# A decode-attention kernel whose last step is written out as a list of its own, and whose first output weights come in uneven pieces

## The chip, the cores and the metric

The kernel runs on one core of one Trainium2 chip. Its time is the device time of one execution in microseconds (us). A profile of one execution gives when every instruction and every DMA packet ran. The engines of the core are PE (the matrix engine; PEld is its loading of weights), DVE (vector), ACT (scalar, activation), POOL and SP, which here does nothing but issue DMAs.

## What is computed

One token goes through an attention block with a cached K and V, and through a gated feed-forward block; a sigmoid gate mixes the two. The cut reference:

```
def _A_ref(x, k_cache, v_cache, wq, wo):          # x 1x1x512, caches 1x32x65536x128, all bf16
    q = (x @ wq).reshape(1, 1, 32, 128).transpose(0, 2, 1, 3)
    scores = jnp.einsum("bhqd,bhkd->bhqk", q, k_cache) * (128 ** -0.5)
    p = softmax(scores)
    o = jnp.einsum("bhqk,bhkd->bhqd", p, v_cache)
    return o.transpose(0, 2, 1, 3).reshape(1, 1, 4096) @ wo

def _B_ref(x, w_gate, w_up, w_down):
    return (silu(x @ w_gate) * (x @ w_up)) @ w_down

g = sigmoid((x * gate_w).sum(-1, keepdims=True))
return g * a + (1 - g) * b
```

There are 32 heads of 65,536 keys and as many values of 128 numbers. K and V together are 1,074 MB, and each number is used once.

## The kernel before

**Tiles.** A head's 65,536 keys are four groups of 16,384; a group is a tile of 128 partitions x 128 keys x 128 numbers, 4,096 KB. Groups are counted through all heads, n = 0 to N-1 = 127, and h = n // 4. K comes in pairs of groups, m = 0 to M-1 = 63, into two slots of 64 KB a partition that are used in turn (`take`, `give`). V has one buffer of the same size, `V_buf`: a head's first pair comes in one DMA, its second pair one group at a time, as each half of the buffer comes free. For the last head the V of groups 124 and 127 goes into the second halves of the two K slots, which are free by then; their first halves hold `wo`, the output weights: heads 0 to 15 in the tile named `wo_early`, the later ones in `wo_late`.

**One group.** `products(n)` on DVE multiplies the K tile by the query (line 260) and adds the halves of each key's 128 products together until 32 are left (line 264, two instructions). `scores(n)` on PE sums these by eight matmuls with the identity (line 273). `fold(n)` on DVE sums the last four (line 288). After a head's four groups `row_max` takes the maximum (DVE line 294, ACT line 296, PE line 298), `exponentials` makes the weights P and their sum by partition (DVE line 303, ACT lines 305 and 307), `total` adds the sum over partitions on PE (line 315), and `weight` makes of it the factor of the head on DVE (lines 320 and 321). `values(n)` on PE multiplies P with the V tile in 32 matmuls (line 329) into one accumulator a head. `head_copy` (ACT line 343) and `head_turn` (PE line 359, ACT line 367) make a column of `oT` of it. At the end `project(h)` on PE multiplies each column with its head's rows of `wo`, in two matmuls of 256 columns into two accumulators (line 385).

**Order.** The order of all instructions on each engine is written out by hand: they run in program order there, and an engine waits where its next instruction's data isn't there. The loop is over i, a pair of groups a step, with `first` for a head's first pair. In a step DVE does `products(2i)`, a `fold` after its first instruction, `products(2i+1)`, another `fold`; PE does the `scores` of this pair and the `values` of the pair two before. In a `first` step the line `tot_ps = total(h - 1)` comes after both `values`, and DVE's `weight(h - 1)`, which reads it, between `products(2i+1)` and the next step's `products`. The last step is i = 63, with conditions of its own (`i == M - 1`), and what is left after it follows the loop.

**DMAs.** SP issues all the large ones in program order (lines 113, 182 and 184). A DMA signals its completion by sixteen marks on a semaphore. Eight semaphores take turns, so SP issues a DMA only when the eighth DMA before it has landed; it also waits until the readers of the place that is overwritten are done. `load_wo` brings heads in groups of four (`QUAD`), 4,096 bytes a partition and group: the 16 early heads in one DMA, the late ones by `LATE_CUTS`. V group 127 is cut into six DMAs (`V_CUTS`).

Of the kernel before, what the change touches and what calls it, by code (L numbers as in the profile page):

```python
# [8 lines left out]
ACT = mybir.ActivationFunctionType  # L9
ALU = mybir.AluOpType  # L10
AXIS = mybir.AxisListType
P = 128
# [3 lines left out]
NB = 128  # L16
# [7 lines left out]
TURNED = 8  # L24
V_CUTS = {3: (0, 64, NB), 2: (0, 64, NB), 1: (0, 32, 64, 96, 112, NB - TURNED, NB)}
EARLY = 16
LATE_CUTS = (EARLY, 24, 28, 30, 32)

GROUPED = 28


@with_exitstack
def kernel(
# [45 lines left out]
    def take(name):  # L79
        slot = free.pop(0)  # L80
        held[name] = slot
        return ring.tile(
            [P, PAIR * Dh], bf16, name=name.split(".")[0], tag=f"slot{slot}"
        )
# [36 lines left out]
    def load_v(n, half=0, spare=None):  # L121
        if n % G == 0 and spare is None:
            view = V_buf.rearrange("p (j d) -> p j d", d=Dh)
            V_tiles[n], V_tiles[n + 1] = view[:, :NB, :], view[:, NB:, :]
            load(view, A_v_cache, n // 2, (0, PAIR))
        else:
            view = V_buf if spare is None else spare
            view = view[:, half * NB * Dh : (half + 1) * NB * Dh]
            V_tiles[n] = view = view.rearrange("p (j d) -> p j d", d=Dh)
            load(view, A_v_cache, n // 2, V_CUTS.get(N - n, (0, NB)), n % 2 * NB)  # L130
# [17 lines left out]
    gval = consts.tile([P, 1], f32, name="gval")  # L148
    rg = consts.tile([P, H], f32, name="rg")
    HD = D // 2  # L150
    a_ps = [psum_a.tile([1, HD], f32, name=f"a{i}_ps") for i in range(2)]

    def queries():
        q_ps = psum_m.tile([P, H], f32, name="q_ps", tag="misc")
# [19 lines left out]
    def load_wo(tile, cuts):  # L174
        t = tile[:, : H * D].rearrange("p (h n) -> p h n", n=D)
        runs = t.rearrange("p (g j) n -> p g (j n)", j=QUAD)
        rows = A_wo.rearrange("(h p) n -> p h n", p=P)
        row_runs = A_wo.rearrange("(g p j) n -> p g (j n)", p=P, j=QUAD)
        for a, b in zip(cuts[:-1], cuts[1:]):
            if b <= GROUPED:  # L180
                a, b = a // QUAD, b // QUAD
                nc.sync.dma_start(out=runs[:, a:b, :], in_=row_runs[:, a:b, :])
            else:
                nc.sync.dma_start(out=t[:, a:b, :], in_=rows[:, a:b, :])
        return t
# [52 lines left out]
    def feed_forward_out(hT, rest):  # L238
        b_ps = psum_m.tile([1, D], f32, name="b_ps", tag="misc")
        for t in range(FT):  # L240
            nc.tensor.matmul(
                b_ps, lhsT=hT[:, t : t + 1], rhs=wd_sb[:, t, :], start=(t == 0), stop=(t == FT - 1)
            )
        b_sb = small.tile([1, D], f32, name="b_sb", tag="row", bufs=1)
        nc.scalar.activation(out=b_sb, in_=b_ps, func=ACT.Copy, scale=rest)
        for i, a in enumerate(a_ps):
            nc.tensor.matmul(
                a, lhsT=ones_f[0:1, 0:1], rhs=b_sb[:, i * HD : (i + 1) * HD], start=True, stop=False
            )

    def width_of(n):
        return FIRST if n < G else WIDTH
# [16 lines left out]
    def scores(n):  # L269
        S = F_tiles[n] = psum_s.tile([P, NB, QUAD], f32, name="S_ps")  # L270
        width = width_of(n)
        for c in range(0, width, QUAD):
            nc.tensor.matmul(  # L273
                S,
                lhsT=ident_b,
                rhs=K_tiles[n][:, :, c : c + QUAD],
                start=(c == 0),
                stop=(c == width - QUAD),
            )
        del K_tiles[n]  # L280
        if n % 2:
            give(f"K_t.{n // 2}")
# [9 lines left out]
    def row_max(h):  # L292
        m = small.tile([P, 1], f32, name="m")
        nc.vector.tensor_reduce(out=m, in_=S_tiles[h], axis=AXIS.X, op=ALU.max)  # L294
        diag = small.tile([P, P], f32, name="diag")
        nc.scalar.activation(out=diag, in_=ident_f, func=ACT.Copy, scale=m)  # L296
        mT_ps = psum_m.tile([P, P], f32, name="mT_ps", tag="misc")
        nc.tensor.matmul(mT_ps, lhsT=ones_f, rhs=diag, start=True, stop=True)  # L298
        return mT_ps

    def exponentials(h, mT_ps):
        top = small.tile([P, 1], f32, name="top")
        nc.vector.tensor_reduce(out=top, in_=mT_ps, axis=AXIS.X, op=ALU.max)  # L303
        bias = small.tile([P, 1], f32, name="bias")
        nc.scalar.activation(out=bias, in_=top, func=ACT.Copy, scale=-scale)  # L305
        P_tiles[h] = small.tile([P, NBH], bf16, name="P_sb")
        nc.scalar.activation(  # L307
            out=P_tiles[h], in_=S_tiles[h], func=ACT.Exp, bias=bias, scale=scale,
            accum_out=rowsum[:, h : h + 1],
        )  # L310
        del S_tiles[h]

    def total(h):
        tot_ps = psum_m.tile([P, 1], f32, name="tot_ps", tag="misc")
        nc.tensor.matmul(tot_ps, lhsT=ones_f, rhs=rowsum[:, h : h + 1], start=True, stop=True)  # L315
        return tot_ps
# [3 lines left out]
        nc.vector.reciprocal(recip, tot_ps)  # L320
        nc.vector.tensor_tensor(out=rg[:, h : h + 1], in0=recip, in1=gval, op=ALU.mult)

    def values(n):
        h, g = divmod(n, G)
        if g == 0:
            O_tiles[h] = psum_o.tile([4, 4 * Dh], f32, name="O_ps")
        end = NB if n < N - 1 else NB - TURNED
        for j in range(0, end, 4):
            nc.tensor.matmul(  # L329
                O_tiles[h],  # L330
                lhsT=P_tiles[h][:, g * NB + j : g * NB + j + 4],
                rhs=V_tiles[n][:, j : j + 4, :],
                start=(g == 0 and j == 0),
                stop=(g == G - 1 and j == end - 4),
            )
# [45 lines left out]
            )  # L381

    def project(h):
        for i, a in enumerate(a_ps):
            nc.tensor.matmul(  # L385
                a,
                lhsT=oT[:, h : h + 1],
                rhs=wo_sb[:, h, i * HD : (i + 1) * HD],
                start=False,
                stop=(h == H - 1),  # L390
            )


    queries()
# [5 lines left out]
    query(0)  # L400

    mT_ps = tot_ps = None
    for i in range(M):
        h, first = i // MH, i % MH == 0
        vector = products(2 * i)
        next(vector)
        if mT_ps is not None:
            exponentials(h - 1, mT_ps)
        if not first:
            fold(2 * i - 1)  # L410
        for _ in vector:
            pass
        if first or i == M - 1:
            scores(2 * i)
        if i >= 2:
            values(2 * i - 4)
            if first or i == M - 1:
                load_v(2 * i - 2 if first else N - 3)
        if not first and i < M - 1:
            scores(2 * i)  # L420
        if i == 0:
            xs = gate_sum()
            eg2 = gate_exp(xs)
        if i >= 2:
            values(2 * i - 3)
            if first or i == M - 1:
                load_v(2 * i - 1 if first else N - 2, 1)
            else:
                load_v(2 * i - 2)
        if mT_ps is not None:  # L430
            tot_ps = total(h - 1)
            mT_ps = None
        if first and i > MH:
            head_turn(h - 2, head_copy(h - 2))
        if i == 1:
            hT = feed_forward_mid(*ff)
            feed_forward_out(hT, rest)
            load_v(0)
        vector = products(2 * i + 1)
        next(vector)  # L440
        fold(2 * i)
        for _ in vector:
            pass
        if i == 0:
            rest = gate_value(eg2)
        if tot_ps is not None:
            weight(h - 1, tot_ps)
            tot_ps = None
        if not first and h + 1 < H:
            query(h + 1)  # L450
        scores(2 * i + 1)
        if i == 0:
            ff = feed_forward_in()
        if i + 2 < M:
            load_k(i + 2)
        elif i + 2 == M:
            spare = take("wo_early.0")
            wo_sb = load_wo(spare, (0, EARLY))
            load_v(N - 4, 1, spare)
        if not first:  # L460
            fold(2 * i + 1)
            mT_ps = row_max(h)
    spare = take("wo_late.0")
    load_v(N - 1, 1, spare)
    exponentials(H - 1, mT_ps)
    for o in range(EARLY):
        project(o)
    tot_ps = total(H - 1)
    head_turn(H - 2, head_copy(H - 2))
    values(N - 4)  # L470
    values(N - 3)
    weight(H - 1, tot_ps)
    wo_sb = load_wo(spare, LATE_CUTS)
    values(N - 2)
    values(N - 1)
    head_turn(H - 1, head_copy(H - 1))
    for h in range(EARLY, H):
        project(h)

    out_sb = small.tile([1, D], bf16, name="out_sb", bufs=1)  # L480
    nc.vector.tensor_copy(out=out_sb[:, :HD], in_=a_ps[0])  # L481
    nc.scalar.activation(out=out_sb[:, HD:], in_=a_ps[1], func=ACT.Copy)
    nc.sync.dma_start(out=out[0], in_=out_sb)


# [28 lines left out]
```

## Time and profile before

| What | us |
|---|---|
| Time, median of 3 runs (2524.94 to 2525.77) | 2525.67 |
| Time of the profiled execution | 2525.51 |
| Its span from the first to the last instruction | 2523.7 |
| PE busy | 1411.6 |
| DVE busy | 2066.2 |
| ACT busy | 115.2 |
| Read from HBM: 1087.64 MB, at 431 GB/s over the span | |
| Last matmul of `project` begins | 2520.9 |
| Output DMA is issued | 2521.65 |

Times within the execution are counted from the start of the span. The difference between the span and the execution's time, 1.8 us, lies around the span.

### The profile page before, as it was taken

What the parts mean: (1) busy time and instruction counts of PE and PEld (TensorE: products, weight loads), DVE (VectorE), ACT (ScalarE), POOL (GpSimd) and SP (SyncE); (2) the same over time, 40 slices, a digit from 0 to 9 for tenths busy, and PEclk for the clock granted to TensorE, in tenths of its full rate; (3) what the DMA queues carried; (4) which work ended last, traced back from release to release, by engine and by line L of the source; (5) the groups of instructions that cost most, each with busy time, mean ns of one, the idle gap of its engine ahead of it and who ended that gap; (6) DMA issues with size and microseconds to landing.
All of it is one profiled execution on the core that took longest, in us unless ns stands there. A gap on an engine that the chain in (4) does not pass through costs nothing.

```text
span 2523.7 us, 13226 instructions
## 1 busy us (share of the span) xinstructions
PE 1411.6 (56%) x5898; PEld 547.1 (22%) x5898; DVE 2066.2 (82%) x648; ACT 115.2 (5%) x348; POOL 0.7 (0%) x6
## 2 busy tenths in 40 slices
PE   3655654646646456555465464664545655546549
PEld 2211221212212122221122121221212222212214
DVE  5898888888888878889888888888788888987883
ACT  0000000000000000000000000000000000000000
POOL 0000000000000000000000000000000000000000
PEclk8777777777767777687787776876867777777779
DMA  9999999999999999999999999999999999999998
GB/s 415 436 434 434 438 432 429 436 433 436 431 431 432 435 442 433 431 427 435 437 434 432 429 437 434 437 435 428 431 437 437 434 433 427 440 431 433 433 430 363
DMA packets 26890, 1088.49 MB, mean 431 GB/s; under 512 B 3153, under 2 KB 3666, under 8 KB 4946
## 3 DMA queue, kind: packets, MB, share of 16 engines
q1 hardware_dynamic: 26546, 1087.65, 99.7%
q8 instruction: 46, 0.75, 0.1%
q14 instruction: 10, 0.08, 0.0%
q10 hardware_dynamic: 288, 0.00, 0.0%
HBM read 1087.64 MB, written 0.00 MB: 431 GB/s over the span
## 4 chain that ended last, share of the span: by engine, by line
DMA 62%; PE 33%; DVE 5%; issue 0%; another core or an unknown queue 0%; ACT 0%; SPq 0%; DVEq 0%; ACTq 0%
DMA V_buf<-in_A_v_cache_dram 58%; PE O_ps L329 29%; DMA K_t<-in_A_k_cache_dram 4%; PE S_ps L273 3%; DVE K_t L260 3%; DVE K_t L264 2%; PE a_ps L385 0%; PE oh_ps L359 0%; DVE S_sb L288 0%; PE tot_ps L315 0%; PE qb_ps L170 0%; DVE m L294 0%; DVE top L303 0%; ACT O_sb L343 0%
## 5 line engine op out<-in xcount | busy, mean ns | idle before, releaser
L260 DVE TENSOR_TENSOR K_t<-K_t,q_sb 128x16384 bf16<-128x16384 bf16 x128 | 1112.1, 8688 | 216.8 <-DMA K_t<-in_A_k_cache_dram 216.8
L329 PE MATMUL O_ps<-V_buf,P_sb 128*4 128x512 bf16 x4032 | 955.9, 400 | 356.3 <-DMA V_buf<-in_A_v_cache_dram 354.9
L264 DVE TENSOR_TENSOR K_t<-K_t 128x8192 bf16<-128x8192 bf16 x252 | 849.3, 3370 | 4.3
L273 PE MATMUL S_ps<-K_t,ident_b 128*128 128x512 bf16 x1056 | 358.6, 499 | 674.9 <-DVE K_t L264 674.9
L329 PEld LDWEIGHTS <-P_sb 128*4 128x4 bf16 x4094 | 358.0, 88 | 973.6 <-issue 507.9
L273 PEld LDWEIGHTS <-ident_b 128*128 128x128 bf16 x1056 | 117.7, 116 | 861.3 <-issue 783.4
L288 DVE TENSOR_REDUCE S_sb<-S_ps 128x128 f32<-128x512 f32 x128 | 87.7, 685 | 117.5 <-PE S_ps L273 117.5
L320 DVE RECIPROCAL recip<-tot_ps 128x1 f32<-128x1 f32 x32 | 5.4, 168 | 79.4 <-PE tot_ps L315 79.4
L376 ACT ACTIVATE oT<-oh_ps,rg 32x1 bf16<-32x1 f32 x112 | 28.6, 255 | 683.5 <-PE oh_ps L359 682.4
L298 PE MATMUL mT_ps<-diag,ones_f 128*128 128x128 f32 x64 | 21.5, 430 | 62.0 <-ACT diag L296 62.0
L172 ACT ACTIVATE q_sb<-qb_ps 128x128 bf16<-128x128 f32 x32 | 8.9, 277 | 933.4 <-PE qb_ps L170 933.4
L359 PE MATMUL oh_ps<-ident_f,O_sb 4*128 4x1 f32 x256 | 33.5, 248 | 0.5 <-ACT O_sb L343 0.5
L298 PEld LDWEIGHTS mT_ps<-diag,ones_f 128*128 128x128 f32 x64 | 13.4, 262 | 89.8 <-ACT diag L296 89.8
L359 PEld LDWEIGHTS oh_ps<-ident_f,O_sb 4*128 4x128 f32 x256 | 30.8, 186 | 1.0 <-ACT O_sb L343 0.5
L481 DVE CAST out_sb<-a_ps 1x256 bf16<-1x256 f32 x1 | 0.4, 413 | 33.2 <-PE a_ps L385 33.2
L296 ACT ACTIVATE diag<-ident_f,m 128x128 f32<-128x128 f32 x32 | 12.8, 401 | 308.0 <-DVE m L294 308.0
L307 ACT ACTIVATE P_sb<-S_sb,bias 128x512 bf16<-128x512 f32 x32 | 23.1, 722 | 1.0
L294 DVE TENSOR_REDUCE m<-S_sb 128x1 f32<-128x512 f32 x32 | 21.9, 686 | 1.1
L305 ACT ACTIVATE bias<-top 128x1 f32<-128x1 f32 x32 | 6.5, 203 | 324.2 <-DVE top L303 324.2
L343 ACT ACTIVATE O_sb<-O_ps 4x512 f32<-4x512 f32 x32 | 18.2, 570 | 27.1 <-PE O_ps L329 27.1
L168 ACT ACTIVATE q_diag<-ident_f,qT 128x128 bf16<-128x128 f32 x32 | 12.8, 400 | 0.4
L315 PEld LDWEIGHTS tot_ps<-rowsum,ones_f 128*128 128x128 f32 x64 | 9.5, 188 | 13.8 <-issue 13.8
(49 smaller groups left out, 104.1 us busy)
## 6 DMA issues: line engine op xcount, KB each, us to landing
V_buf<-in_A_v_cache_dram SPq DMA_DIRECT2D x62, 4096.0 KB, 23.4
K_t<-in_A_k_cache_dram SPq DMA_DIRECT2D x4, 4096.0 KB, 32.2
V_buf<-in_A_v_cache_dram SPq DMA_DIRECT2D x4, 2048.0 KB, 22.4
V_buf<-in_A_wq_dram SPq DMA_DIRECT2D x1, 4096.0 KB, 12.5
wo_early<-in_A_v_cache_dram SPq DMA_DIRECT2D x1, 4096.0 KB, 35.7
wo_late<-in_A_v_cache_dram SPq DMA_DIRECT2D x3, 1024.0 KB, 26.2
wo_early<-in_A_wo_dram SPq DMA_DIRECT2D x1, 2048.0 KB
V_buf<-in_B_w_gate_dram SPq DMA_DIRECT2D x1, 1792.0 KB, 54.5
```

Source lines behind the costliest of these rows:

```text
L168: nc.scalar.activation(out=diag, in_=ident_f, func=ACT.Copy, scale=qT[:, h : h + 1])
L260: yield nc.vector.tensor_tensor(out=K, in0=K, in1=q_rep, op=ALU.mult)
L264: yield nc.vector.tensor_tensor(out=K[:, :, 0:half], in0=K[:, :, 0:half], in1=K[:, :, half : 2 * half], op=ALU.add,)
L273: nc.tensor.matmul(S, lhsT=ident_b, rhs=K_tiles[n][:, :, c : c + QUAD], start=(c == 0), stop=(c == width - QUAD),)
L288: nc.vector.tensor_reduce(out=S_tiles[h][:, g * NB : (g + 1) * NB], in_=F_tiles.pop(n), axis=AXIS.X, op=ALU.add)
L294: nc.vector.tensor_reduce(out=m, in_=S_tiles[h], axis=AXIS.X, op=ALU.max)
L298: nc.tensor.matmul(mT_ps, lhsT=ones_f, rhs=diag, start=True, stop=True)
L307: nc.scalar.activation(out=P_tiles[h], in_=S_tiles[h], func=ACT.Exp, bias=bias, scale=scale, accum_out=rowsum[:, h : h + 1],)
L329: nc.tensor.matmul(O_tiles[h], lhsT=P_tiles[h][:, g * NB + j : g * NB + j + 4], rhs=V_tiles[n][:, j : j + 4, :], start=(g == 0 and j == 0) ...
L343: nc.scalar.activation(out=dst, in_=src, func=ACT.Copy)
L359: nc.tensor.matmul(oh_ps, lhsT=O_sb[:, c * Dh : (c + 1) * Dh], rhs=ident_f[0:4, c : c + 1], start=(c == 0 and not turned), stop=(c == 3),)
L376: nc.scalar.activation(out=oT[part * A : (part + 1) * A, g * QUAD + j : g * QUAD + j + 1], in_=oh_ps[j * A : (j + 1) * A, :], func=ACT.Cop ...
```

## The change

```diff
 EARLY = 16
-LATE_CUTS = (EARLY, 24, 28, 30, 32)
+MIDDLE = 20
+LATE_CUTS = (MIDDLE, 24, 28, 30, 32)
+UNEVEN, SHARE = (0, 1), 125
...
-    a_ps = [psum_a.tile([1, HD], f32, name=f"a{i}_ps") for i in range(2)]
+    a_ps = psum_a.tile([1, D], f32, name="a_ps")
...
             if b <= GROUPED:
                 a, b = a // QUAD, b // QUAD
+                for g in range(a, b):
+                    if g in UNEVEN:
+                        for part in (slice(0, SHARE), slice(SHARE, P)):
+                            nc.sync.dma_start(out=runs[part, g, :], in_=row_runs[part, g, :])
+                        a = g + 1
                 nc.sync.dma_start(out=runs[:, a:b, :], in_=row_runs[:, a:b, :])
...
-    def values(n):
+    def values(n, start=0, stop=NB):
...
-        for j in range(0, end, 4):
+        for j in range(start, min(stop, end), 4):
...
     def project(h):
-        for i, a in enumerate(a_ps):
-            nc.tensor.matmul(
-                a,
-                lhsT=oT[:, h : h + 1],
-                rhs=wo_sb[:, h, i * HD : (i + 1) * HD],
...
+        nc.tensor.matmul(
+            a_ps,
+            lhsT=oT[:, h : h + 1],
+            rhs=(wo_early if h < EARLY else wo_late)[:, h, :],
...
-    for i in range(M):
+    for i in range(M - 1):
...
+        if mT_ps is not None:
+            tot_ps = total(h - 1)
+            mT_ps = None
         if i >= 2:
             values(2 * i - 4)
...
-        if mT_ps is not None:
-            tot_ps = total(h - 1)
-            mT_ps = None
...
+    spare = take("wo_early.0")
+    wo_early = load_wo(spare, (0, EARLY))
+    load_v(N - 4, 1, spare)
+    vector = products(N - 2)
+    next(vector)
+    fold(N - 3)
+    for _ in vector:
+        pass
+    scores(N - 2)
+    values(N - 6)
+    load_v(N - 3)
+    vector = products(N - 1)
+    next(vector)
+    fold(N - 2)
+    for _ in vector:
+        pass
+    values(N - 5, 0, NB // 2)
+    scores(N - 1)
     spare = take("wo_late.0")
+    wo_late = load_wo(spare, (EARLY, MIDDLE))
+    values(N - 5, NB // 2, 3 * NB // 4)
+    fold(N - 1)
+    mT_ps = row_max(H - 1)
+    values(N - 5, 3 * NB // 4)
+    load_v(N - 2, 1)
     load_v(N - 1, 1, spare)
+    load_wo(spare, LATE_CUTS)
     exponentials(H - 1, mT_ps)
-    for o in range(EARLY):
-        project(o)
+    O_sb = head_copy(H - 2)
+    for h in range(EARLY // 2):
+        project(h)
+    head_turn(H - 2, O_sb)
+    values(N - 4)
     tot_ps = total(H - 1)
-    head_turn(H - 2, head_copy(H - 2))
-    values(N - 4)
+    weight(H - 1, tot_ps)
+    for h in range(EARLY // 2, EARLY):
+        project(h)
     values(N - 3)
-    weight(H - 1, tot_ps)
-    wo_sb = load_wo(spare, LATE_CUTS)
+    for h in range(EARLY, MIDDLE):
+        project(h)
     values(N - 2)
     values(N - 1)
     head_turn(H - 1, head_copy(H - 1))
-    for h in range(EARLY, H):
+    for h in range(MIDDLE, H):
         project(h)
```

In words: the loop ends one step earlier, and the last step stands after it, without conditions. In the loop, `total` of the head before now comes ahead of the two `values` on PE's queue. In the last step `values(123)` is cut into a half and two quarters, with `scores(127)` and the matmul of `row_max` between them. `project` is one matmul of 512 columns into one accumulator, and is done for heads 0 to 7, 8 to 15, 16 to 19 and 20 to 31 at four places instead of 0 to 15 and 16 to 31 at two. The weights of heads 16 to 19 are loaded by themselves, ahead of V groups 126 and 127. The early weights, one DMA of 2,048 KB before, are five DMAs: for each of the first two groups of heads one of 125 partitions (500 KB) and one of three (12 KB), then one of 1,024 KB.

More of the change, by code (lines that the diff above doesn't have):

```diff
@@ L245, in feed_forward_out @@
         nc.scalar.activation(out=b_sb, in_=b_ps, func=ACT.Copy, scale=rest)
-        for i, a in enumerate(a_ps):
-            nc.tensor.matmul(
-                a, lhsT=ones_f[0:1, 0:1], rhs=b_sb[:, i * HD : (i + 1) * HD], start=True, stop=False
-            )
+        nc.tensor.matmul(a_ps, lhsT=ones_f[0:1, 0:1], rhs=b_sb, start=True, stop=False)
     def width_of(n):
@@ L383, in project @@
     def project(h):
-        for i, a in enumerate(a_ps):
-            nc.tensor.matmul(
-                a,
-                lhsT=oT[:, h : h + 1],
-                rhs=wo_sb[:, h, i * HD : (i + 1) * HD],
-                start=False,
-                stop=(h == H - 1),
-            )
+        nc.tensor.matmul(
+            a_ps,
+            lhsT=oT[:, h : h + 1],
+            rhs=(wo_early if h < EARLY else wo_late)[:, h, :],
+            start=False,
+            stop=(h == H - 1),
+        )
     queries()
@@ L412 @@
             pass
-        if first or i == M - 1:
+        if first:
             scores(2 * i)
+        if mT_ps is not None:
+            tot_ps = total(h - 1)
+            mT_ps = None
         if i >= 2:
             values(2 * i - 4)
-            if first or i == M - 1:
-                load_v(2 * i - 2 if first else N - 3)
-        if not first and i < M - 1:
+            if first:
+                load_v(2 * i - 2)
+        if not first:
             scores(2 * i)
@@ L425 @@
             values(2 * i - 3)
-            if first or i == M - 1:
-                load_v(2 * i - 1 if first else N - 2, 1)
+            if first:
+                load_v(2 * i - 1, 1)
             else:
                 load_v(2 * i - 2)
-        if mT_ps is not None:
-            tot_ps = total(h - 1)
-            mT_ps = None
         if first and i > MH:
@@ L455 @@
             load_k(i + 2)
[L456 to L459, printed above, removed]
         if not first:
@@ L476 @@
     head_turn(H - 1, head_copy(H - 1))
-    for h in range(EARLY, H):
+    for h in range(MIDDLE, H):
         project(h)
     out_sb = small.tile([1, D], bf16, name="out_sb", bufs=1)
-    nc.vector.tensor_copy(out=out_sb[:, :HD], in_=a_ps[0])
-    nc.scalar.activation(out=out_sb[:, HD:], in_=a_ps[1], func=ACT.Copy)
+    nc.vector.tensor_copy(out=out_sb[:, :HD], in_=a_ps[:, :HD])
+    nc.scalar.activation(out=out_sb[:, HD:], in_=a_ps[:, HD:], func=ACT.Copy)
     nc.sync.dma_start(out=out[0], in_=out_sb)
```

## The prediction

> **What bounds the kernel now.** I read the page's slices first. The rows show when DMA, DVE and PE are busy, in 40 slices of 63 us:
>
> ```profile
> PE   3655654646646456555465464664545655546549
> DVE  5898888888888878889888888888788888987883
> DMA  9999999999999999999999999999999999999998
> GB/s 415 436 434 434 438 432 429 436 433 436 431 431 432 435 442 433 431 427 435 437 434 432 429 437 434 437 435 428 431 437 437 434 433 427 440 431 433 433 430 363
> ```
>
> The DMA engines are full from end to end; only the last slice is lower, 363 GB/s, and there PE is at 9 and DVE at 3. So the body costs what the 1,088 MB cost, and only the end is open to a reordering. Next the windows of the end (length; busy time and count of PE, PEld, DVE, ACT, POOL; granted clock; DMA share, GB/s):
>
> ```profile
> 2490.00:2495.00 5.00, 5.00 (x25) 1.99 (x24) 0.00 (x0) 0.00 (x0) 0.00 (x0) 1.00 1.00 429
> ...
> 2505.00:2510.00 5.00, 5.00 (x25) 1.96 (x23) 0.00 (x0) 0.00 (x0) 0.00 (x0) 1.00 1.00 411
> 2510.00:2515.00 5.00, 5.00 (x25) 1.96 (x23) 0.00 (x0) 0.00 (x0) 0.00 (x0) 1.00 0.66 254
> ```
>
> PE is busy without a hole, at the full granted clock, while DMA runs dry from 2510. PE ends last. The chain of waits (start, duration, what) says how PE came to be so late:
>
> ```profile
> 2431.22 14.05 PE O_ps L329 x64
> 2445.26 0.33 PE tot_ps L315 x2
> 2445.59 0.02 issue
> 2445.62 0.18 DVE recip L320
> 2445.79 0.02 issue
> 2445.82 0.16 DVE rg L321
> 2445.98 8.60 DVE K_t L260
> ...
> 2461.89 3.57 PE S_ps L273 x8
> 2465.46 13.96 PE O_ps L329 x64
> 2479.42 1.85 PE S_ps L273 x8
> ...
> 2483.20 0.49 PE mT_ps L298 x2
> 2483.68 3.58 PE a_ps L385 x32
> 2487.27 0.31 PE tot_ps L315 x2
> 2487.58 0.98 PE oh_ps L359 x8
> 2488.56 27.30 PE O_ps L329 x126
> ```
>
> Read it backwards: from 2488.56 only PE's own work; before that, twice, DVE's products; and DVE began those late because `weight(30)` sat waiting for `total(30)`, which PE had queued behind 64 `values` matmuls. The timeline gives that wait its length:
>
> ```profile
> 2445.62 0.17 DVE L320 RECIPROCAL recip<-tot_ps 128x1 f32<-128x1 f32 x1 [2.24 <-PE tot_ps L315]
> ```
>
> **The change, part by part.**
>
> *`total` ahead of `values`.* The sum that it needs was ready at 2421.94 (ACT line 307: 2421.75 + 0.19), and PE ends `scores(124)` at 2431.14, so `total` runs at 2431.2 instead of 2445.2, and DVE's 2.24 us are gone: `products(126)` begins at 2443.67 instead of 2445.89. Its K half has landed by 2440.83, the other by 2450.50 where it is needed at 2459.5, so DMA doesn't take the gain back. The 0.31 us of `total` now delay `values(120)` and the V load behind it by 0.3; the chain's V DMA landed at 2431.17, so PE has next to no wait there to hide it in, but the DMA queue has: the load issued at 2438.39 starts moving bytes when the K half in front ends on the first DMA engines, at 2441.93. If that cover were gone it would cost 0.3. In the other 31 heads the same wait goes (79.4 us in 32, most of it the same 2.2 us); there DVE then waits for K (216.8 us in all in line 260), as DMA sets the pace. Worth nothing in the body, **2.22 us at the end**.
>
> *The last step's order.* DVE now ends the products of 127 at 2477.70 - 2.22 = 2475.48. PE: `scores(126)` from 2459.66, 3.57 (half clock, as now: idle before it); 48 matmuls, 10.5, to 2473.7; 1.8 idle; `scores(127)` 2475.52 to 2477.4. Before, all 64 stood in front of it and made it wait until 2479.42. From there to the matmul of the maximum it takes 3.78 (2479.42 to 2483.20) on DVE and ACT, so that starts at 2479.30; eight `values` matmuls (1.75 at 14.05/64) fit in beside it. The idle 1.8 us shouldn't lower the clock: between 2481.27 and 2483.20 PE idles 1.9 now, and the clock stays 1.00. Against the old 2483.20 this is 3.90 earlier, with the last eight matmuls of `values(123)` still to do, +1.75. Net -2.15 of which 2.22 is the wait above: the weaving by itself swaps one idle stretch (1.93) for another (1.8) and gains nothing. If half speed came back, eight matmuls would cost 1.7 more.
>
> *`project`.* 64 matmuls in 3.58 + 3.60 = 7.18 become 32 of 512 columns; the nearest row is line 329 with 512 columns, 27.30/126 = 0.217 to 0.219 each: 7.0, so -0.2. The moved ACT and DVE work has slack: the weights P are ready near 2481.2 (1.4 after the maximum), `head_copy(30)` near 2482.2 for a `head_turn` at 2483.3, and `weight(31)` (0.33) finds DVE idle. Moving heads 16 to 19 forward shortens what comes after the last V, but not PE's sum. Both halves of the output row now come from one accumulator; DVE's copy took 0.41 and ACT's 0.37 beside each other. Side by side again, 0; one after the other, +0.4. I take 0: they already overlap by all but 0.1.
>
> *Five DMAs more.* SP issues take 0.33 to 0.5 each and SP sits idle between; 2 us more ahead of V group 124, which is then issued at 2450.8 instead of 2448.86, while the queue holds V until 2461.33 on the first engines. With eight semaphores in turn, each later DMA waits for another one: worked along the list, the last is issued when the second piece of V 127 lands, near 2508 to 2510 (2508.91 now), and the third piece of V 127 waits for group 124, at 2482 to 2485, where DMA has groups 125 and 126 still to move. None runs dry. Nothing on the path.
>
> *The uneven pieces.* This no row shows: every large load has 128 partitions. The sixteen landing marks of each DMA tell what matters, though. The marks of the last weights lie at 2511.1 to 2511.5 for six engines, 2512.2 and 2514.8 for two, 2517.4 to 2518.9 for eight: spread 7.8 us. For group 125 it is 8.7, five marks within 0.3 in front; at 100 us it was 1.6. Eight engines fell behind by the code loads (the page's 46 packets of the instruction queue). The sum of the two groups, 1,024 KB, takes 2.47 an engine when spread over 16 (2,048 KB of `wo_early`: 2461.33 to 2466.27, 4.94). On e engines it takes 39.5/e: 2.5 on 16, 7.9 on 5, 39.5 on one. The output DMA, of one partition, has two marks instead of 16, so a shape can confine a DMA to few engines. If shares stay equal, as with 128 partitions, 125 rows go to five engines or one. Bounds: spread over 16, nothing changes; all on one engine, +37. I take five, the middle; then what counts is whether they lead or lag: a lead of 7 to 8.7 us holds 7.9 - 2.5 = 5.4 more, and the other engines run 2.5 ahead of now. I take leading ones, by the five marks that stand in front; the three-partition pieces (12 KB) add under 1 us to engines with as much in hand.
>
> [...]
>
> *Does DMA keep up with the earlier PE?* PE from 2479.30: 0.49 + 1.75 + eight heads 1.75 + `head_turn` 0.98, so `values(124)` begins at 2484.3; group 126's second half is wanted at 2504.8, 127's third quarter at 2511.8, the last weights at 2518.4. Landings now: 2484.5; 2504.0 and 2511.3, each +1.2 for the 512 KB of weights moved ahead; 2518.9. That is even to 0.7 late; with the laggards 2.5 ahead it is some 2 us of cover everywhere.
>
> **Sum.** From 2479.30: 0.49 + 1.75 + 20 heads 4.38 + 0.31 + 0.98 + 27.30 + 0.72 (wait and copy) + 1.05 + 12 heads 2.63 = 39.61, end of PE at 2518.9 instead of 2521.23: 2.3 less. The profiled execution took 2525.51, hence **2523.2**; its median lies 0.16 above, so 2523.4 as a median; I say 2523.3.
>
> **The rivals.**
>
> *The uneven pieces fall on lagging engines.* These carry the end: group 124 lands 5.4 later, 2489.9, against a need at 2484.3, and the last weights at 2524.3. Two heads (0.44) and what follows the last matmul now (2523.7 - 2521.23 = 2.47) make 2527.2, with 1.8 around the span **2529.0**, slower by 0.14%. It decides as soon as a chosen engine's lag, plus 5.4, passes the 8.6 of the slowest by more than 2. For: eight of sixteen lag, and five picked at random would nearly always hold one. Against: the lead is itself in a block of five, which a count of five may match.
>
> *They are spread evenly, so the change of pieces does nothing.* Then PE waits at 127's third quarter, 0.7, and the end is **2524.0**.
>
> *All rows on one engine.* A leading one marks V 124 at 2476.0 + 37 = 2513.0, 28.7 after PE's need, and all of PE's rest follows: **2552**, slower by 1.0%. For: the output row. Against: 125 is not one.
>
> *DVE's gain doesn't arrive,* because `products(126)` meets another wait or PE's clock drops in the new pause: **2525.5**. Against: K's landings have 2.8 and 9 us to spare.
>
> **How the numbers follow.** Forecast 64%, its own range 2522.3 to 2524.2; lagging engines 13%; evenly spread 8%; gain lost 9%; one engine 3%; a gain beyond what I can account for 3%. The range 2521.8 to 2527.3 holds all but the two slow ones and the last. What a measurement can tell from no change is about 0.2%, 5 us: the forecast is 0.09% and falls inside. Faster by more: 4%. Slower by more: the one engine and a third of the lagging case at its upper edge, 7%. Within: 89%.
>
> **What would show it.** Right: `total` before `values` in every head and no DVE wait at line 320; line 260 for group 126 near 2443.7; the last V matmul near 2515, `project` ending near 2519; the marks of the last weights within some 3 us of each other, the last near 2516.5. Wrong: PE idle before `values(124)` with the early tile's DMA as releaser, a mark spread that grew to 13 us, or half clock in `values(123)`.

## The result, and the profile after

The changed kernel takes 2535.08 us (median of 5 runs, 2534.07 to 2535.42) against 2525.57 us before: 9.5 us more, ratio 1.0035, interval 1.0024 to 1.0046. A gain of 2.3 us had been forecast; the range ended at 2527.3. The profiled execution has a span of 2531.9 us against 2523.7.

The slices of the whole span put the loss at the end. The rate of the last two slices is lower, 410 and 327 GB/s, where before only the last was:

```profile
DMA  9999999999999999999999999999999999999998
GB/s 414 435 441 434 430 432 432 437 435 434 433 428 434 439 435 431 430 433 442 430 430 434 435 431 437 434 432 433 430 439 434 430 433 434 433 434 433 433 410 327
```

The windows of the end (length; busy time and count of PE, PEld, DVE, ACT, POOL; granted clock; DMA share, GB/s), first of the kernel before:

```profile
2460.00:2465.00 5.00, 3.11 (x8) 1.00 (x7) 5.00 (x2) 0.00 (x0) 0.00 (x0) 0.50 0.95 406
2465.00:2470.00 5.00, 5.00 (x24) 1.81 (x23) 5.00 (x1) 0.00 (x0) 0.00 (x0) 0.95 1.01 429
2470.00:2475.00 5.00, 5.00 (x25) 1.99 (x24) 5.00 (x3) 0.00 (x0) 0.00 (x0) 1.00 1.06 450
2475.00:2480.00 5.00, 5.00 (x24) 1.87 (x23) 2.67 (x2) 0.00 (x0) 0.00 (x0) 1.00 0.94 406
```

And of the changed kernel:

```profile
2455.00:2460.00 5.00, 0.17 (x1) 0.10 (x1) 4.97 (x3) 0.00 (x0) 0.00 (x0) 0.50 1.00 433
2460.00:2465.00 5.00, 5.00 (x14) 1.46 (x13) 5.00 (x1) 0.00 (x0) 0.00 (x0) 0.56 1.06 331
2465.00:2470.00 5.00, 5.00 (x25) 1.97 (x24) 5.00 (x3) 0.00 (x0) 0.00 (x0) 1.00 1.04 256
2470.00:2475.00 5.00, 0.92 (x5) 0.26 (x3) 4.97 (x2) 0.00 (x0) 0.00 (x0) 0.96 0.93 218
2475.00:2480.00 5.00, 3.39 (x9) 1.00 (x9) 0.64 (x1) 0.00 (x0) 0.00 (x0) 0.50 1.06 341
2480.00:2485.00 5.00, 5.00 (x20) 1.68 (x19) 0.52 (x1) 0.00 (x0) 0.00 (x0) 0.85 0.97 414
```

The DMA share stays near 1.00 while the rate falls to half. So the engines don't starve; each packet takes longer. Here it is the share beside the rate that shows contention; the share alone, as in the slices' row of nines, would have hidden it.

PE feels it at three places in the timeline (start, duration, what, and in brackets the idle time before and what ended it):

```profile
2476.61 6.00 PE L334 MATMUL O_ps<-V_buf,P_sb 128*4 128x512 bf16 x16 [5.69 <-DMA V_buf<-in_A_v_cache_dram]
...
2493.28 7.07 PE L334 MATMUL O_ps<-wo_early,P_sb 128*4 128x512 bf16 x32 [1.89 <-DMA wo_early<-in_A_v_cache_dram]
...
2521.25 3.18 PE L334 MATMUL O_ps<-wo_late,P_sb 128*4 128x512 bf16 x14 [0.28 <-DMA wo_late<-in_A_v_cache_dram]
```

The first wait is for V group 123, whose load was issued before the uneven pieces: a DMA that is ahead in the queue was slowed by one behind it. The chain of waits shows the same. Where the old chain ended in PE's own work from 2488.56 on, the new one runs through two DMAs:

```profile
2451.30 41.94 DMA wo_early<-in_A_v_cache_dram
2493.24 0.02 issue
2493.26 27.95 DMA wo_late<-in_A_v_cache_dram
2521.21 0.04 issue
2521.25 3.20 PE O_ps L334 x14
```

DVE's wait at `weight` is gone, as meant: the row had 2.24 us of idle time in brackets, and now has none.

```profile
2443.56 0.16 DVE L325 RECIPROCAL recip<-tot_ps 128x1 f32<-128x1 f32 x1
```

### The profile page after: what moved, and what is told of

The parts are those of the page before. It is cut to its first block, busy times and chain, and to the rows that moved or that the text cites. A ratio compares the mean times of both kernels' runs of the same rounds, so it can differ in the third digit from the quotient of the medians.

```text
span 2531.9 us, 13162 instructions
## 1 busy us (share of the span) xinstructions
PE 1415.1 (56%) x5864; PEld 553.9 (22%) x5864; DVE 2063.4 (81%) x648; ACT 115.4 (5%) x348; POOL 0.7 (0%) x6
## 4 chain that ended last, share of the span: by engine, by line
DMA 52%; PE 26%; DVE 21%; issue 0%; SPq 0%; another core or an unknown queue 0%; ACT 0%; DVEq 0%; ACTq 0%
DMA K_t<-in_A_k_cache_dram 49%; PE O_ps L334 18%; DVE K_t L265 12%; DVE K_t L269 9%; PE S_ps L278 7%; DMA wo_early<-in_A_v_cache_dram 2%; PE oh_ps L364 1%; DMA wo_late<-in_A_v_cache_dram 1%; DVE top L308 0%; PE tot_ps L320 0%; PE a_ps L389 0%; DVE S_sb L293 0%; SPq L188 0%; DVEq L265 0%
## 5 line engine op out<-in xcount | busy, mean ns | idle before, releaser
L265 DVE TENSOR_TENSOR K_t<-K_t,q_sb 128x16384 bf16<-128x16384 bf16 x128 | 1112.1, 8688 | 295.4 <-DMA K_t<-in_A_k_cache_dram 295.4
L334 PE MATMUL O_ps<-V_buf,P_sb 128*4 128x512 bf16 x4032 | 965.7, 402 | 359.5 <-DMA V_buf<-in_A_v_cache_dram 359.5
L364 PEld LDWEIGHTS oh_ps<-ident_f,O_sb 4*128 4x128 f32 x256 | 30.8, 186 | 14.1 <-issue 13.5
L320 PEld LDWEIGHTS tot_ps<-rowsum,ones_f 128*128 128x128 f32 x64 | 20.1, 316 | 12.1 <-issue 9.2
L325 DVE RECIPROCAL recip<-tot_ps 128x1 f32<-128x1 f32 x32 | 5.1, 160 | 13.5 <-PE tot_ps L320 13.5
```

The costliest lines, as they stand in the source:

```text
L265: yield nc.vector.tensor_tensor(out=K, in0=K, in1=q_rep, op=ALU.mult)
L334: nc.tensor.matmul(O_tiles[h], lhsT=P_tiles[h][:, g * NB + j : g * NB + j + 4], rhs=V_tiles[n][:, j : j + 4, :], start=(g == 0 and j == 0) ...
L364: nc.tensor.matmul(oh_ps, lhsT=O_sb[:, c * Dh : (c + 1) * Dh], rhs=ident_f[0:4, c : c + 1], start=(c == 0 and not turned), stop=(c == 3),)
```

## The experiments

Each kernel was timed beside runs of the kernel before; ratios are to those. The three kernels with loads added at their end ran once, for the trace alone. The theory from this profile: while the pieces of 125 partitions move, they lengthen the packets of all DMA engines. The rivals: the new order and its waits cost the time; or one of the five engines lags and only its share is late; or few engines with long lists are to blame, whatever partitions they write.

**The order without the pieces.**

```diff
-UNEVEN, SHARE = (0, 1), 125
+UNEVEN, SHARE = (), 125
```

> The new order with the early weights in one DMA again. Shared slowdown (the pieces of 125 partitions make the packets of all engines longer while they move, 1213 to about 2150 ns for 32 KB): without them nothing is lost and the new order gives its 2.3 us, 2523 to 2524. Order at fault (moved waits or SP's new sequence cost most of the 9.5 us): 2530 or more.

2525.18 us beside 2526.30, ratio 0.9995 (0.9986 to 1.0004): no loss, and no gain that can be told from none; the span is 0.3 us shorter, where 2.3 had been expected. The order isn't what costs. Its DMA rate keeps up in the stretch that fell:

```profile
2465.00:2470.00 5.00, 5.00 (x25) 1.96 (x23) 5.00 (x3) 0.00 (x0) 0.00 (x0) 1.00 0.98 417
2470.00:2475.00 5.00, 4.54 (x22) 1.71 (x20) 4.97 (x2) 0.00 (x0) 0.00 (x0) 1.00 1.06 450
```

**The pieces without the order.** The loop of the new `load_wo` in the old kernel, nothing else.

```diff
+                for g in range(a, b):
+                    if g in UNEVEN:
+                        for part in (slice(0, SHARE), slice(SHARE, P)):
+                            nc.sync.dma_start(out=runs[part, g, :], in_=row_runs[part, g, :])
+                        a = g + 1
```

> The old order with the uneven pieces alone. Shared slowdown: V group 124 lands some 8 us later and PE waits for it, so 2532 to 2536; packets of 32 KB beside the pieces near 2150 ns. Order at fault: 2525 to 2527. Lagging engines (one of the five is behind and its share queues, other engines untouched): packets stay at 1213 ns, time 2528 to 2530.

2533.51 us beside 2526.30, ratio 1.0028 (1.0018 to 1.0039): a loss of 7.2 us, which within the intervals can be all of the change's 9.5. The pieces carry it. 32 KB packets that start between 2463 and 2473 take 2146 ns on average.

**Other cuts.** 64 and 64 partitions, and 120 and 8, in the whole change:

```diff
-UNEVEN, SHARE = (0, 1), 125
+UNEVEN, SHARE = (0, 1), 64
```

> The whole change, but the two groups cut into 64 and 64 partitions, which all 16 engines can share evenly. If the slowdown comes of few engines with long lists: none here, packets stay at 159 ns (4 KB) and 1213 ns (32 KB), time as with the new order alone, 2523 to 2524. If it comes of engines that write other partitions than in a load of 128: packets lengthen here too, 4 KB beyond 200 ns, and the time lies 2 to 8 us above the new order alone.

> The whole change, but cut into 120 and 8 partitions. 120 goes evenly on 15 engines with 8 rows each, as many as in a load of 128. If few engines with long lists are the cause: next to none here, 2523 to 2524.5. If other partitions than in a load of 128 are the cause: the packets lengthen as in the change, and the time lies several us above the new order alone.

64 and 64: 2532.06 us, ratio 1.0022 (1.0013 to 1.0031). 120 and 8: 2531.28 us, 1.0020 (1.0011 to 1.0029). Some 7 and 6 us above the order alone. In the trace the loads of 64 have sixteen landing marks each, so all engines work at them, and the loss is still there: few engines with long lists are not the cause. The load of 120 in the run of loads by themselves has sixteen marks too, which fits one for each of 15 engines and one half a microsecond after the issue, as the pieces of 125 have one beside five.

**The same number of DMAs, by columns.** Each group in two DMAs of 128 partitions and half the columns.

```diff
-                        for part in (slice(0, SHARE), slice(SHARE, P)):
-                            nc.sync.dma_start(out=runs[part, g, :], in_=row_runs[part, g, :])
+                        for part in (slice(0, 2 * D), slice(2 * D, 4 * D)):
+                            nc.sync.dma_start(out=runs[:, g, part], in_=row_runs[:, g, part])
```

> The whole change, but each of the two groups cut in two by columns (128 partitions, 2 KB each) instead of by partitions: as many DMAs, the same bytes, the same partitions to an engine as in every other load. Shared slowdown by foreign partitions: nothing of it here, time as the order alone within 0.5 us. If five DMAs instead of one, or the waits that move along the eight semaphores, are the cause: 5 us or more above it.

2525.56 us beside 2525.96, ratio 0.9998 (0.9989 to 1.0007). Five DMAs instead of one and the shifted semaphores cost nothing that can be seen; the cut by partitions does. Where an engine writes partitions that another engine writes in a load of 128, this is called a crossing below. The traces name neither the engine of a packet nor its partitions, so that a crossing is what lengthens the packets is the author's reading of the runs. The packets of these kernels, read from the trace's DMA records for starts between 2463 and 2473 (mean, least and greatest in ns), and the bytes moved from 2460 to 2480:

```
kernel             4 KB packets     32 KB packets        MB
before             159 (159-159)    1213 (1213-1213)    8.45
order alone        159 (159-159)    1213 (1213-1213)    8.45
by columns         159 (159-159)    1213 (1213-1213)    8.37
the change         277 (219-402)    2148 (2028-2561)    5.73
pieces alone       282 (216-561)    2146 (2040-2315)    5.60
64 and 64          252 (174-464)    1795 (1420-2698)    5.93
120 and 8          234 (159-352)    1720 (1366-2182)    6.16
one group only     244 (161-439)    1819 (1389-2253)    6.77
```

The 32 KB packets belong to V, not to the pieces, and with pieces even the shortest of them takes longer than 1213: no V packet that starts in these ten us is spared. That two loads are in flight together is not enough: in the first three rows packets of 4 and of 32 KB also move beside each other, at 159 and 1213.

**Half the dose.**

```diff
-UNEVEN, SHARE = (0, 1), 125
+UNEVEN, SHARE = (0,), 125
```

> The whole change, but only the first group in pieces of 125 and 3. If the loss is the time in which such pieces move: half of that of two groups, 4 to 5 us above the order alone. If it is a loss for entering that state once: nearly all of it.

2528.28 us beside 2525.96, ratio 1.0009 (1.0000 to 1.0018): some 3 above the order alone; 4 to 5, half of the whole, had been expected. The 32 KB packets are back within 12 ns of 1213 from 2474 on with one group and from 2481 on with two, when the last of the five engines is done: of the first piece of 125, four marks come at 2468.9 to 2469.7 and the fifth at 2474.9 (2474.7 with one group); of the second, four by 2476.7 and the fifth at 2481.4. The fifth engine is some 5 us behind the other four, and its last 100 KB keep the crossing alive alone: with two groups the 20 packets of 32 KB that start from 2478 to 2480, after the other four are done, take 1329 to 1828 ns. V group 124's last mark is 2484.76 in the order alone, 2487.75 with one group and 2493.24 with two; the next to last is 2487.22 and 2489.51. So what nearly all engines lose, 2.5 and 4.8 us, does go with the number of groups; with two, the fifth engine adds 3.7 by being last. PE meets this differently in the two kernels. With two groups it waits for group 123 and again for group 124. With one it does not wait for group 124: it had waited 4.06 us for group 123, until 2473.85, its next 16 matmuls took 6.41 us at half clock (0.54 granted from 2475 to 2480), and it begins `values(124)` at 2489.09 with the data there, 4.3 later than in the order alone.

**Loads by themselves.** Seven loads at the end of the order alone, each waiting for the one before.

```diff
+    again = wo_early[:, :EARLY, :].rearrange("p (g j) n -> p g (j n)", j=QUAD)
+    source = A_wo.rearrange("(g p j) n -> p g (j n)", p=P, j=QUAD)
+    for lo, hi in ((0, 128), (0, 64), (0, 32), (0, 16), (0, 120), (0, 125), (0, 128)):
+        nc.sync.dma_start(out=again[lo:hi, :, :], in_=source[lo:hi, 0 : EARLY // QUAD, :])
```

> The order alone, and at its end, when nothing else is moving, seven more loads of early weights one after the other into a place that is free by then, of 128, 64, 32, 16, 120, 125 and 128 partitions with 16 KB each. [...] If an engine's own rate is all that counts (159 ns for 4 KB): 128 takes 5 us to move, 64 takes 2.5, 32 takes 1.3, 16 takes 0.6, 120 on 15 engines 5, 125 on five engines 16. [...]

The DMA issues of that stretch (KB, us from issue to landing; the first row holds the last load of 128, since the first was issued before this stretch and still had late engines before it; the load of 125 has no landing in this view, its last mark came 17.5 after its issue):

```profile
wo_early<-in_A_wo_dram SPq DMA_DIRECT2D x1, 2048.0 KB, 7.7
wo_early<-in_A_wo_dram SPq DMA_DIRECT2D x1, 2000.0 KB
wo_early<-in_A_wo_dram SPq DMA_DIRECT2D x1, 1920.0 KB, 12.1
wo_early<-in_A_wo_dram SPq DMA_DIRECT2D x1, 1024.0 KB, 7.7
wo_early<-in_A_wo_dram SPq DMA_DIRECT2D x1, 512.0 KB, 4.5
wo_early<-in_A_wo_dram SPq DMA_DIRECT2D x1, 256.0 KB, 4.1
```

64 partitions take as long as 128 (7.7 us), with half the bytes; 16 nearly as long as 32 (4.1 against 4.5); 120 take longer than 128 (12.1 against 7.7). An engine's own rate of 159 ns a packet doesn't give these times; by the author's reading engines that write such partitions stand in each other's way. The load of 125, alone, runs its packets at 159 ns, 26 GB/s for each of five engines: by itself it is slow only for want of engines. A crossing needs somebody to cross. 64 partitions move at about half the rate of 128 (178 against 393 GB/s in the next experiment).

**Reading or writing.** The same megabyte into 64 partitions, and into 128 with half as much each; then pairs in flight.

```diff
+    nc.sync.dma_start(out=x[0:64], in_=source[0:64, G4, :])
+    nc.sync.dma_start(out=x[:, :, C2], in_=halves[0, :, G4, :])
...
+    for _ in range(2):
+        nc.sync.dma_start(out=x, in_=source[:, G4, :])
+        nc.sync.dma_start(out=y[0:64], in_=source[0:64, G4, :])
```

> The order alone, and at its end, when nothing else moves, loads of early weights into places that are free: 2,048 KB into 128 partitions; then 1,024 KB into 64; then the same 1,024 KB of HBM into 128 partitions with half as much each. Then pairs that are in flight together: 2,048 KB into 128 partitions beside 1,024 KB into 64, twice, and the same beside 1,024 KB into 128, twice. If the way into SBUF is shared by the engines of a load of 64: its 1,024 KB take 7.7 us from issue to landing as before, and the same bytes into 128 about 4.7. If reading these rows is what is slow: 7.7 for both. For the pairs, if mixing costs no more than the shared ways: the pair with 64 lands about 2.5 us later than the pair with 128 only. If mixing slows engines whose ways nobody else uses: clearly more than that, and all packets of 4 KB beyond 200 ns.

The windows while only the 64, then only the 128 partitions are written:

```profile
2528.00:2531.00 3.00, 0.00 (x0) 0.00 (x0) 0.00 (x0) 0.00 (x0) 0.00 (x0) 0.50 0.90 178
2534.00:2536.00 2.00, 0.00 (x0) 0.00 (x0) 0.00 (x0) 0.00 (x0) 0.00 (x0) 0.50 1.02 393
```

The last mark came 7.6 after the issue into 64 and 5.2 into 128 (4.7 was the author's estimate); steady packets took 330 ns for 4 KB there, 84 for 2 KB here. The same bytes of HBM in 7.6 and in 5.2 us, so reading isn't what is slow: it is the writing. In the pairs the engines were within 1 us of each other, and the two loads ran one after the other, the 128 at 159 ns and the 64 at 330: counted from the landing of the load in front, the 64 partitions landed 5.0 us later and the 128 2.5, as if nothing mixed. So these pairs did not try mixing: in the kernel, where packets did lengthen, the engines are at different places in the queue, up to 8.6 us apart.

**One load beside another.** A load of 128 partitions (32 KB packets) beside five others.

```diff
+    nc.sync.dma_start(out=x[0:127, 0, :], in_=source[0:127, 0, :])
+    nc.sync.dma_start(out=V_tiles[N - 4], in_=rows[:, :NB, :])
```

> The order alone, and at its end, when nothing else moves, a load of 128 partitions (4,096 KB in packets of 32 KB, 1213 ns each when undisturbed) beside five other loads issued just ahead of it: one of 128 partitions; one of 125 (1,000 KB, five engines); one of 8 neighbouring partitions, 64 to 71 (256 KB); one of 127 (508 KB, one engine); one of 128 again. If only engines whose way into SBUF is crossed are slowed: beside the 8 partitions most packets stay at 1213 ns and a few take twice as long or more, and beside the single engine at most one packet in sixteen is longer at a time. If a crossing slows all engines: nearly all packets beside 125 partitions near 2100 ns and beside the single engine near 1450, as in the change, and those beside the 8 partitions longer too.

The 127 partitions went to one engine (two marks, the second 32.5 us after the issue) and so made the cleanest case. Alone, from 2571 to 2575, its 4 KB packets took 159 ns. Once the load of 128 came beside it, from 2579 to 2587, its own took 274 on average, and all 89 of the others' 32 KB packets took longer than 1213: 1475 on average, none under 1378. The window of that stretch has a full share at a lower rate:

```profile
2579.00:2587.00 8.00, 0.00 (x0) 0.00 (x0) 0.00 (x0) 0.00 (x0) 0.00 (x0) 0.50 1.09 379
```

One engine with the load of 127 slowed the fifteen others by a fifth. From 2597 to 2603 the same engine was still behind, by a whole load, but it now wrote its own share of a load of 128 while the fifteen wrote the next one: all 78 packets took 1213. So the engine out of step cost nothing as such; what it wrote did. Beside 125 partitions the load in front, from 2535 to 2540, had packets of 1928 to 2308, 2158 on average, as in the change; those of the load behind (2544 to 2546) took 1432 to 1819. The part with 8 partitions told nothing, since its neighbour started only when it was nearly done.

**Two accumulators again.** Not about the loss: in the order alone the two copies of the output row ran in a row.

```diff
-    a_ps = psum_a.tile([1, D], f32, name="a_ps")
+    a_ps = [psum_a.tile([1, HD], f32, name=f"a{i}_ps") for i in range(2)]
...
+        for i, a in enumerate(a_ps):
+            nc.tensor.matmul(
+                a,
```

> The order alone, with two accumulators of 256 columns again instead of one of 512. In the order alone DVE's copy ran at 2520.55 and ACT's after it at 2520.99; in the kernel before they ran beside each other. If the one accumulator is what puts them in a row: the copies overlap again, 0.4 us less than the order alone. If project in two matmuls is slower: no gain or a loss of 0.1.

2524.73 us beside 2525.96, ratio 0.9995 (0.9986 to 1.0004), the same ratio as with one accumulator; 0.4 us is less than this interval can tell. The timelines show the overlap; first one accumulator, then two:

```profile
2520.55 0.41 DVE L513 CAST out_sb<-a_ps 1x256 bf16<-1x256 f32 x1 [27.96 <-PE a_ps L389]
2520.99 0.37 ACT L514 ACTIVATE out_sb<-a_ps 1x256 bf16<-1x256 f32 x1 [2.86 <-DVE out_sb L513]
```

```profile
2520.99 0.41 DVE L518 CAST out_sb<-a_ps 1x256 bf16<-1x256 f32 x1 [28.52 <-PE a_ps L394]
2521.10 0.37 ACT L519 ACTIVATE out_sb<-a_ps 1x256 bf16<-1x256 f32 x1 [2.44 <-PE a_ps L394]
```

With one accumulator ACT is released by DVE's copy; with two, by PE. From the landing of the V that PE waits for last to the end of ACT's copy it is 8.54 us with one (2512.82 to 2521.36) and 8.12 with two (2513.35 to 2521.47): in the trace the 0.4 are there. No version beats the kernel before by what can be measured.

## Why the prediction was wrong

**The step that failed** is the pricing of the uneven pieces. It bounded them by how the bytes could be spread, from "spread over 16, nothing changes" to "all on one engine, +37", and took five leading engines at no cost. The count was right: each piece of 125 has six marks instead of the sixteen of a load of 128, one half a microsecond after the issue and five at landing. What failed is that all of this kept the rate of a packet fixed, at 159 and 1213 ns. The nearest rows could only have one rate, since every large load in the kernel wrote 128 partitions; that is a reason to leave the rate open, not to fix it. In the runs the rate changed for everyone: 2.72 MB less moved from 2460 to 2480 than in the order alone (5.73 against 8.45), 6.3 us at 432 GB/s. The last V piece that PE waits for landed at 2521.21 instead of the 2512.82 of the order alone, 8.4 us later, and the spans of these two executions differ by 8.5.

The prediction's own signs of being wrong were there: PE idle for 1.89 us before `values(124)` with the early tile's DMA as releaser, marks spread over 12.1 us for group 124 and 14.6 for group 123, and half clock in `values(123)` (0.50 granted from 2475 to 2480), after PE's wait of 5.69 us.

**The first rival** said slower, but had the wrong mechanism for most of it. Four of the five engines did lead. The fifth lay behind, and its double share holds the last mark of group 124 3.7 us behind the next. But it was not one of the rearmost eight: those finish group 123 at 2472.87 or later, and 25 packets of even 159 ns would take them past 2474.89. It seems to be the one in the middle, 4.3 us behind the first in the kernel before (2465.67 against 2461.33). 4.3 and 5.4 pass the 8.6 of the slowest by 1.1, less than the 2 that the prediction asked for, so with packets at their old length this lag would not have decided. And loads of 64, shared by all sixteen, lose 7 us. The rival's price, 2529.0, carried only the lag.

**`total` ahead of `values`** came as forecast: `products(126)` began at 2443.71 in the order alone (forecast 2443.67), the matmul of the maximum at 2479.40 (forecast 2479.30). In the other heads the wait went too (79.4 us in 32 at that line became 13.5 in one in the change), and DVE's waits for K grew from 216.8 to 295.4 us: worth nothing in the body, as said.

**The sum for the order**, without the pieces, gave too much. PE ended at 2520.52 instead of 2518.9, 1.6 later. It waited three times for V in the order alone, 0.40, 0.24 and 0.34 us, together 0.98, much as the second rival (2524.0) had it for evenly spread weights; the rest lies in many small steps and was not followed up. After PE's end the copies in a row cost the 0.4 that was named as a bound and taken as 0. The span came out at 2523.4, 0.3 under the kernel before.

**`project`** in one matmul: twelve heads took 2.69 us, 0.224 each, against 0.225 in two matmuls. In the chain of the kernel with one group all 32 took 7.10 us against 7.18 before, so at most half of the 0.2 us of the sum was there.

**Five DMAs more**: nothing that can be told, as forecast; the cut by columns shows it.

## What to carry to other kernels

Load over all 128 partitions, and divide a transfer along the columns when it has to be divided: here the cut by columns left the 32 KB packets beside it at 1213 ns, while pieces of 125, 120 and 64 partitions with their rests lengthened them to between 1720 and 2148 on average, and a load of 127 to 1475. Where a change alters the shape of a transfer, ask what it does to the transfers beside it as well as when it lands itself. And in a profile set the DMA share beside the rate: here a full share at half the rate was contention.

## What the runs showed of the hardware

The slowdown reaches all engines: the one with the load of 127 partitions lengthened every 32 KB packet of the fifteen others, 1213 to 1475 ns on average, though it moved only 4 KB in 274 ns, some 15 GB/s. If it slowed only one neighbour at a time, at most one packet in sixteen would have been longer at a time, by the author's estimate. Loads of 64 and of 16 partitions took as long or nearly as long as those of 128 and 32 (7.7 us each, 4.1 against 4.5); what the engines share was not found out.

The sixteen engines drift apart over the run, from 0.5 to 8.6 us in the kernel before: eight of them fall back in steps of about 1.4 us, and the lengths of the 46 code loads (16 KB each, on the page's instruction queue) repeat with a period of eight (947, 879, 879, 935, 929, 922, 961 and 962 ns, then from the start, to within 9 ns), so these eight seem to take them. With that lag the pieces ran beside other loads; in the pairs above, with the engines within 1 us, the loads only followed each other. A load on one engine did the same, since the others went on to the next load: beside that of 127 partitions, whose second mark came 32.5 us after its issue.
